# A fused attention, mixture-of-experts and dense kernel: ScalarE's three readings of q are ordered behind the eviction of the value product three pairs ahead

## The chip, the cores and the metric

The kernel is one program on one core of a Trainium2 chip, compiled once. The metric is the device time of one execution in microseconds. The kernel before takes 913.57 us, the median of three runs (913.28 to 913.73). The engines are TensorE (PE, its weight loads PEld), VectorE (DVE), ScalarE (ACT), GpSimd (POOL) and SyncE (SP), which issues most of the transfers.

## What is computed

Three layers follow each other: attention with a compressive memory, a mixture of experts with one expert per token, and a dense layer with a squared relu. The change touches the attention alone, for B=4, H=8, S=576, D=64:

```python
scores = scale * np.matmul(q, k.transpose(0, 1, 3, 2))       # scale = 1/8, causal mask
a = softmax(scores)
local = np.matmul(a, v)                                       # the value product
q_p = np.where(q > 0, q, np.exp(q) - 1.0) + 1.0               # phi(q)
mem_out = (q_p @ M_prev) / (q_p @ z_prev + 1e-6)
attn_out = g * mem_out + (1 - g) * local
```

## The kernel before

**Pairs.** The attention works on 16 pairs of heads (`pair`, 4 batches of 4). Each pair is a Python generator in four parts: "prep" (loads of k and q, their splitting in high and low parts), "front" (scores and their softmax), "back" (turning the weights `a`, the value product, mixing with the memory), "end" (turning the result, routing logits, store). At step t of the main loop, pair t+2 is in prep, t+1 in front, t in back and t-1 in end, interleaved by the table `PLAN`. The program is then put in order by a scheduler that works with estimated durations; `tc.issue_after(x)` around an instruction forbids it to place that instruction ahead of x on its engine.

**Preparation.** For each pair ScalarE copies k into `kh` (L188) and makes `qh` = q/8 (L198), `ex` = exp(q) (L199) and `rq` = relu(q) (L200) from `qraw`, which has two buffers; `qh`, `ql`, `ex` and `rq` have one each. VectorE makes the rest `ql` (L201) and `qpad` = min(ex, 1) + rq (L226), which is phi(q). GpSimd makes `kl` = k - kh (L191) and copies the last 64 queries (`qlasth`, `qlastl`, L214). SyncE copies `qh`, `ql`, `kh` and `kl` into the stacked operands `q2`, `k2`, `qlz`.

**Scores.** `scores((3,))`, `scores((1, 0))` and `scores((2,))` each fill two PSUM banks (tiles `sc3x`, `sc1x`, `sc2x`, one for each head; all are `sc` in the trace). VectorE takes the row maximum (`negm`, L275), ScalarE the exponential (`a`, L278). The last 64 queries of both heads go through `psl` (L287, `al` L288). There are six rotating banks for all tiles made by `bank()`, so each one waits for the eviction of the sixth before it.

**Back.** TensorE turns the weights (`ptl`, `pt`, L76), evicted by `evac` (L171) into `aTs`, ScalarE or VectorE by the table `EV`. The value product is `pva` (L363, 20 matmuls, the columns from 128 on) and `pvb` (L368). ScalarE evicts `pva` into `pvs`, VectorE `pvb`; `c.value` is the eviction of `pva` of the pair that was in back last. The result is turned (`ppt`), scaled by `cl` (L340, L342) into `tl` (L381) and GpSimd adds the memory's part to it (`xb`, L383).

In batch 0 alone, `qh` of a pair is ordered behind `c.value`, which is then the eviction of the pair three places ahead of it; `ex` and `rq` are free everywhere, and `qh` is in the other batches.

Of the kernel before, what the change touches and what calls it, by code (L numbers as in the profile page):

```python
# [14 lines left out]
AF = mybir.ActivationFunctionType  # L15
# [121 lines left out]
def attention(tc, c, q, k, v, x_dram, pools):  # L137
    nc = tc.nc
# [34 lines left out]
    def pair(b, hp, lgT):  # L173
# [6 lines left out]
        def load(nm, src, pool, nb):  # L180
            t = pool.tile([P, S], F32, tag=nm + "raw", name=nm + "raw", bufs=nb)
            nc.sync.dma_start(out=t, in_=src[b, hp])
            return t

        ks = load("k", k, fr, 3)
        qs = load("q", q, fr, 2)
# [7 lines left out]
        ql = fr.tile([P, S], F32R, tag="ql", name="ql", bufs=1)  # L194
        ex = fr.tile([P, S], F32, tag="ex", name="ex", bufs=1)
        rq = fr.tile([P, S], F32, tag="rq", name="rq", bufs=1)
        with tc.issue_after(c.value.ins) if c.value and b == 0 else nullcontext():
            nc.scalar.mul(qh, qs, 0.125)  # L198
        nc.scalar.activation(ex, qs, AF.Exp)  # L199
        nc.scalar.activation(rq, qs, AF.Relu)  # L200
        nc.vector.scalar_tensor_tensor(out=ql, in0=qs, scalar=0.125, in1=qh.bitcast(F32), op0=ALU.mult, op1=ALU.subtract)  # L201
        stacked = b or hp >= NPLAIN

# [237 lines left out]

    order = list(pairs())
    gens = [pair(*o) for o in order]
    n = len(gens)

# [949 lines left out]
```

## Time and profile before

| | |
|---|---|
| median of three runs | 913.57 us (913.28 to 913.73) |
| the profiled execution's own time | 913.89 us |
| its span | 912.2 us, 14430 instructions |
| granted TensorE clock over the span | 0.996 |
| PE / PEld busy | 891.9 us (98%) / 727.3 us (80%) |
| DVE / ACT / POOL busy | 558.4 (61%) / 469.7 (51%) / 191.1 us (21%) |
| the attention's value products | first begins at 26.2 us, the 16th at 220.6 us |

Engine times are shares of a span that holds three stages with different limits; the attention is roughly its first quarter, the rest is experts and dense layer. A busy PE includes the modelled ends of pipelined matmuls, so short waits inside a chain of transposes do not show as idle time. An instruction's time on DVE or POOL includes the time for which it stands at the engine and is kept from its memory port. A releaser is inferred: where an instruction waited for several things, the one that came last is named.

### The profile page before, as it was taken

How to read it: one execution, taken by the hardware profiler on the slowest of the kernel's cores; microseconds unless marked ns; L12 is line 12 of the kernel's file. 1: busy time of each engine (PE TensorE's matmuls, PEld its weight loads, DVE VectorE, ACT ScalarE, POOL GpSimd, SP SyncE). 2: the span in 40 equal slices, each digit the busy share in tenths (PEclk: the TensorE clock that was granted, in tenths of full speed). 3: DMA queues.
4: the chain of work that ended last, by engine and by line, in shares of the span. 5: the costliest groups of instructions: out<-in, count | busy, mean ns of one | idle time of the engine just before them, and what ended most of it. 6: DMA issues, size and time to landing. Idle time of an engine off the chain costs nothing. (4 is left out here: it accounts for less than half of the span.)

```text
span 912.2 us, 14430 instructions
## 1 busy us (share of the span) xinstructions
PE 891.9 (98%) x5208; PEld 727.3 (80%) x5208; DVE 558.4 (61%) x1083; ACT 469.7 (51%) x934; POOL 191.1 (21%) x265
## 2 busy tenths in 40 slices
PE   8899999999989999999999999999999999999998
PEld 5677777777557889889898788888888888888897
DVE  7787988887586887786778699332223222222232
ACT  6788787864445765566566578432222222222232
POOL 6234233423002133054413004130002000100000
PEclk8999999999999999999999999999999999999999
DMA  7987778655647978856761674120002000100010
GB/s 202 219 196 191 192 191 208 157 134 176 202 152 260 353 284 294 295 195 195 247 239 70 238 238 172 35 93 12 12 12 70 1 1 1 46 1 1 3 44 24
DMA packets 81932, 128.97 MB, mean 141 GB/s; under 512 B 9473, under 2 KB 34049, under 8 KB 81857
## 3 DMA queue, kind: packets, MB, share of 16 engines
q1 hardware_dynamic: 76144, 108.86, 39.1%
q0 software_dynamic: 5712, 19.14, 6.4%
q8 instruction: 43, 0.70, 0.3%
q14 instruction: 33, 0.26, 0.1%
HBM read 109.10 MB, written 15.99 MB: 137 GB/s over the span
## 5 line engine op out<-in xcount | busy, mean ns | idle before, releaser
L1232 DVE SCALAR_TENSOR_TENSOR r<-phf,r 128x512 f32<-128x512 f32 (+1 forms) x64 | 40.0, 625 | 176.9 <-ACT r L1230 176.9
L1230 ACT ACTIVATE r<-phf 128x512 f32<-128x512 f32 (+1 forms) x79 | 43.8, 554 | 185.9 <-PE phf L82 181.6
L886 DVE TENSOR_TENSOR wc<-raw,wc 128x1024 fp32r<-128x1024 f32 x91 | 118.3, 1343 | 14.4 <-ACT wc L884 12.9
L80 PE MATMUL phf<-yT,w 128*128 128x512 f32 (+1 forms) x320 | 119.9, 375 | 0.0
L82 PE MATMUL phf<-yT,w 128*128 128x512 f32 (+1 forms) x320 | 118.2, 369 | 1.0 <-DVE w L1140 1.0
L81 PE MATMUL phf<-yT,w 128*128 128x512 f32 (+1 forms) x320 | 117.9, 369 | 0.0
L884 ACT CAST wc<-raw 128x1024 fp32r<-128x1024 f32 x108 | 106.3, 1056 | 18.9 <-DMA raw<-in_w_dram 5.3
L80 PE MATMUL po<-w,gT 128*128 128x512 f32 x256 | 99.8, 391 | 0.3 <-PEq L1102 0.3
L81 PE MATMUL po<-w,gT 128*128 128x512 f32 x256 | 99.8, 390 | 0.0
L82 PE MATMUL po<-w,gT 128*128 128x512 f32 x256 | 92.8, 391 | 0.0
L278 ACT ACTIVATE a<-sc,negm 128x512 f32<-128x512 f32 (+3 forms) x128 | 66.6, 529 | 12.8 <-DVE negm L275 12.8
L80 PE MATMUL py<-wc,hT 128*128 128x512 f32 x176 | 69.9, 397 | 0.2 <-ACT hT L923 0.2
L81 PE MATMUL py<-wc,hT 128*128 128x512 f32 x176 | 68.9, 392 | 0.8 <-DVE wc L886 0.8
L82 PEld LDWEIGHTS phf<-yT,w 128*128 128x128 f32 x320 | 60.2, 188 | 11.7 <-DVE w L1140 1.4
L80 PEld LDWEIGHTS phf<-yT,w 128*128 128x128 f32 x320 | 60.2, 188 | 11.5
L82 PE MATMUL py<-wc,hT 128*128 128x512 f32 x176 | 68.9, 391 | 0.4 <-DVE hT L924 0.4
L81 PEld LDWEIGHTS phf<-yT,w 128*128 128x128 f32 x320 | 60.3, 188 | 10.1
L1237 DVE TENSOR_TENSOR gT<-r,gT 128x512 fp32r<-128x512 f32 x63 | 43.5, 691 | 40.2 <-ACT gT L1236 39.8
L275 DVE TENSOR_REDUCE negm<-sc 128x1 f32<-128x512 f32 (+3 forms) x128 | 55.2, 484 | 19.2 <-PE sc L272 19.1
L886 POOL TENSOR_TENSOR wc<-raw,wc 128x1024 fp32r<-128x1024 f32 x17 | 44.2, 2600 | 90.2 <-ACT wc L884 82.5
L80 PEld LDWEIGHTS po<-w,gT 128*128 128x128 f32 x256 | 48.1, 188 | 10.8 <-issue 0.7
L82 PEld LDWEIGHTS po<-w,gT 128*128 128x128 f32 x256 | 48.0, 188 | 10.3
(358 smaller groups left out, 1953.4 us busy)
## 6 DMA issues: line engine op xcount, KB each, us to landing
raw<-in_w_dram SPq DMA_DIRECT2D x64, 1024.0 KB, 5.4
q<-qh SPq DMA_DIRECT2D x60, 128.0 KB, 2.6
kraw<-in_k_dram SPq DMA_DIRECT2D x16, 288.0 KB, 5.3
qraw<-in_q_dram SPq DMA_DIRECT2D x16, 288.0 KB
vts<-in_v_dram SPq DMA_DIRECT2D x16, 256.0 KB, 3.5
x_dram<-xb SPq DMA_DIRECT2D x16, 256.0 KB, 4.6
k<-kh SPq DMA_DIRECT2D x30, 128.0 KB, 3.2
k<-kl SPq DMA_DIRECT2D x30, 128.0 KB, 2.5
```

Source lines behind the costliest of these rows:

```text
L80: nc.tensor.matmul(out, lhsT=lh, rhs=rh, start=start, stop=False)
L81: nc.tensor.matmul(out, lhsT=lh, rhs=rl, start=False, stop=False)
L82: return nc.tensor.matmul(out, lhsT=ll, rhs=rh, start=False, stop=stop)
L275: nc.vector.tensor_reduce(out=negm[:, h, j:j + 1], in_=psv, axis=AX.X, op=ALU.max, negate=True)
L278: nc.scalar.activation(a[:, h, aoff[j]:aoff[j] + nk], psv, AF.Exp, bias=negm[:, h, j:j + 1], accum_out=ssum[:, h, j:j + 1])
L884: nc.scalar.copy(wc[:, 0, ks], raw[:, ks])
L886: eng.tensor_sub(wc[:, 1, ks], raw[:, ks], wc[:, 0, ks].bitcast(F32))
L1230: nc.scalar.activation(r[:, 0:nt], ph[:, 0:nt], AF.Relu)
L1232: nc.vector.scalar_tensor_tensor(out=r[:, 0:nt], in0=ph[:, 0:nt], scalar=0.0, in1=r[:, 0:nt], op0=ALU.max, op1=ALU.mult)
L1237: nc.vector.tensor_sub(gT[:, 1, 0:nt], r[:, 0:nt], gT[:, 0, 0:nt].bitcast(F32))
```

## The change

The order that held for `qh` in batch 0 now holds for `qh`, `ex` and `rq` in every batch:

```diff
@@ -194,10 +194,10 @@
         ex = fr.tile([P, S], F32, tag="ex", name="ex", bufs=1)
         rq = fr.tile([P, S], F32, tag="rq", name="rq", bufs=1)
-        with tc.issue_after(c.value.ins) if c.value and b == 0 else nullcontext():
+        with tc.issue_after(c.value.ins) if c.value else nullcontext():
             nc.scalar.mul(qh, qs, 0.125)
-        nc.scalar.activation(ex, qs, AF.Exp)
-        nc.scalar.activation(rq, qs, AF.Relu)
+            nc.scalar.activation(ex, qs, AF.Exp)
+            nc.scalar.activation(rq, qs, AF.Relu)
```

No instruction is added or removed; the scheduler places them anew. 13 of the 16 pairs have such a `c.value` to wait for. Below is ScalarE around the value product of the fourth pair (`pva_1097`); `qh_1178`, `kh_1156` and `ex_1180` are of the seventh pair, `ex_1382` and `rq_1383` of the eighth. Before:

```order
L198 ACTIVATE qh_1178<-qraw_1154 128x576
L199 ACTIVATE ex_1382<-qraw_1356 128x576
L200 ACTIVATE rq_1383<-qraw_1356 128x576
L171 COPY pvs1_119<-pva_1097 128x448
L188 CAST kh_1156<-kraw_1152 128x576
L278 ACTIVATE a_962,ssum_961<-sc20_1119,negm_960 128x384
L278 ACTIVATE a_962,ssum_961<-sc21_1120,negm_960 128x384
L171 COPY aTs0_128<-pt00_1203 128x512
```

And with the change:

```order
L171 COPY pvs1_119<-pva_1097 128x448
L198 ACTIVATE qh_1178<-qraw_1154 128x576
L199 ACTIVATE ex_1180<-qraw_1154 128x576
L200 ACTIVATE rq_1181<-qraw_1154 128x576
L188 CAST kh_1156<-kraw_1152 128x576
L278 ACTIVATE a_962,ssum_961<-sc20_1119,negm_960 128x384
L278 ACTIVATE a_962,ssum_961<-sc21_1120,negm_960 128x384
L171 COPY aTs0_128<-pt00_1203 128x512
```

The eviction moved ahead of three activations that now stand between it and `kh`; `ex` and `rq` are of the same pair as `qh`, no longer one pair ahead.

VectorE follows. Around the same value product, before:

```order
L226 SCALAR_TENSOR_TENSOR qpad0_115<-ex_1180,rq_1181 128x576
L355 TENSOR_TENSOR xm_1083<-pm0_1084,cm_1079 128x384
L354 RECIPROCAL cm_1079<-cm_1079 128x4
L355 TENSOR_TENSOR xm_1083<-pm3_1091,cm_1079 128x256
L201 SCALAR_TENSOR_TENSOR ql_1179<-qraw_1154,qh_1178 128x576
L171 COPY pvs1_119<-pvb_1098 128x128
L407 TENSOR_TENSOR lgT_205<-lgT_205,plg_1113 128x160
L275 TENSOR_REDUCE negm_960<-sc20_1119 128x1
L275 TENSOR_REDUCE negm_960<-sc21_1120 128x1
L381 TENSOR_TENSOR tl_1137<-ppt0_1132,cl_1080 128x512
L381 TENSOR_TENSOR tl_1142<-ppt4_1140,cl_1080 128x128
L171 COPY aTs0_128<-ptl_1145 128x2x2x64
```

And with the change:

```order
L407 TENSOR_TENSOR lgT_205<-lgT_205,plg_1113 128x160
L201 SCALAR_TENSOR_TENSOR ql_1179<-qraw_1154,qh_1178 128x576
L275 TENSOR_REDUCE negm_960<-sc20_1119 128x1
L275 TENSOR_REDUCE negm_960<-sc21_1120 128x1
L381 TENSOR_TENSOR tl_1137<-ppt0_1132,cl_1080 128x512
L381 TENSOR_TENSOR tl_1142<-ppt4_1140,cl_1080 128x128
L226 SCALAR_TENSOR_TENSOR qpad0_115<-ex_1180,rq_1181 128x576
L171 COPY aTs0_128<-ptl_1145 128x2x2x64
L340 SCALAR_TENSOR_TENSOR cl_1282<-ssum_961,gneg_235 128x10
L342 RECIPROCAL cl_1282<-cl_1282 128x10
L275 TENSOR_REDUCE negm_1162<-sc30_1214 128x1
```

`ql` moved behind the copy of the logits, and `qpad` from ahead of `xm` to between `tl` and the eviction of `ptl`; behind it stand `cl` and the maximum of the next scores. TensorE's order in these pairs is the same as before, and so is GpSimd's (`qlasth`, `qlastl`, `kl`, `xb`).

## Rows read from the trace of the kernel before

**Rows 1.** Waits, 0 to 240 us: engine, line, releaser: us in total, times, longest.
```profile
ACT ex L199 <- DMA qraw<-in_q_dram: 9.6, 7, 2.9
PE ppt L76 <- ACT pvs L171: 5.2, 4, 2.2
```
**Rows 2.** Timeline of PE, 67 to 83 us: start us, us, what, count.
```profile
67.38 2.70 PE L363 MATMUL pva<-aTs,vts 128*64 128x448 f32 x20
...
71.27 0.34 PE L267 MATMUL sc<-kh,qlz 128*128 128x384 f32 x1
...
72.75 0.38 PE L80 MATMUL psl<-kh,qlasth 128*128 128x288 f32 x1
73.03 0.77 PE L76 MATMUL pt<-ident,a 128*128 128x128 f32 x5
...
77.05 0.39 PE L254 MATMUL sc<-k,q 128*128 128x256 f32 x2
...
79.85 2.70 PE L363 MATMUL pva<-aTs,vts 128*64 128x448 f32 x20
```
**Rows 3.** Timeline of ACT, 68 to 77 us; in brackets the idle time before.
```profile
68.71 0.69 ACT L198 ACTIVATE qh<-qraw 128x576 fp32r<-128x576 f32 x1
69.95 0.68 ACT L199 ACTIVATE ex<-qraw 128x576 f32<-128x576 f32 x1 [0.55 <-DMA qraw<-in_q_dram]
70.54 0.67 ACT L200 ACTIVATE rq<-qraw 128x576 f32<-128x576 f32 x1
71.11 0.51 ACT L171 COPY pvs<-pva 128x448 f32<-128x448 f32 x1
71.64 0.67 ACT L188 CAST kh<-kraw 128x576 fp32r<-128x576 f32 x1
72.31 0.58 ACT L278 ACTIVATE a<-sc,negm 128x384 f32<-128x384 f32 x1
...
75.55 0.69 ACT L278 ACTIVATE a<-sc,negm 128x512 f32<-128x512 f32 x1 [0.80 <-DVE negm L275]
```
**Rows 4.** Timeline of DVE, 69 to 81 us.
```profile
69.49 0.82 DVE L201 SCALAR_TENSOR_TENSOR ql<-qraw,qh 128x576 fp32r<-128x576 f32 x1 [0.17 <-DMA qraw<-in_q_dram]
...
71.72 1.02 DVE L275 TENSOR_REDUCE negm<-sc 128x1 f32<-128x384 f32 x2 [0.62 <-PE sc L272]
72.66 0.88 DVE L381 TENSOR_TENSOR tl<-ppt,cl 128x512 f32<-128x512 f32 x2
73.45 0.41 DVE L171 COPY aTs<-ptl 128x256 f32<-128x256 f32 x1
73.78 0.16 DVE L340 SCALAR_TENSOR_TENSOR cl<-ssum,gneg 128x10 f32<-128x10 f32 x1
73.98 0.22 DVE L342 RECIPROCAL cl<-cl 128x10 f32<-128x10 f32 x1
74.83 1.29 DVE L275 TENSOR_REDUCE negm<-sc 128x1 f32<-128x512 f32 x2 [0.63 <-PE sc L272]
...
80.02 0.75 DVE L226 SCALAR_TENSOR_TENSOR qpad<-ex,rq 128x576 f32<-128x576 f32 x1
```
**Rows 5.** Timeline of POOL, 72 to 76 us.
```profile
72.45 1.41 POOL L191 TENSOR_TENSOR kl<-kraw,kh 128x576 fp32r<-128x576 f32 x1 [1.47 <-issue]
73.82 1.71 POOL L383 TENSOR_TENSOR xb<-tl,xm 128x512 f32<-128x512 f32 x2
```
**Rows 6.** Timelines of POOL and DVE at 14 us and at 216 us.
```profile
14.03 1.40 POOL L191 TENSOR_TENSOR kl<-kraw,kh 128x576 fp32r<-128x576 f32 x1 [1.85 <-ACT kh L188]
...
14.50 1.54 DVE L201 SCALAR_TENSOR_TENSOR ql<-qraw,qh 128x576 fp32r<-128x576 f32 x1
...
215.90 1.69 POOL L383 TENSOR_TENSOR xb<-tl,xm 128x512 f32<-128x512 f32 x2 [9.53 <-DVE tl L381]
...
216.08 1.13 DVE L340 SCALAR_TENSOR_TENSOR cl<-ssum,gneg 128x10 f32<-128x10 f32 x1
```
**Rows 7.** Timeline of PE in a pair with no `psl` product, 132 to 142 us.
```profile
132.79 2.70 PE L363 MATMUL pva<-aTs,vts 128*64 128x448 f32 x20
...
141.87 0.44 PE L254 MATMUL sc<-k,q 128*128 128x256 f32 x2
```

## The prediction

> **What bounds the kernel now.** I read the waits first. In the attention ScalarE waits 9.6 us in front of `ex` for loads of q, and TensorE waits 5.2 us in front of `ppt` for the eviction of the value product [rows 1]. The two belong together: before the change `ex` and `rq` of the next pair stand between the value product and its eviction, and a late load of q holds all three. That is what the change undoes.
>
> Then I read one undisturbed pair in the timeline, engine by engine, because the page's busy share of TensorE hides short waits. The fourth value product ends at 67.38 + 2.70 = 70.08 us [rows 2]. From there a chain runs that is not TensorE's own. `kh` begins at 71.64 [rows 3], when the last score product that reads its buffer has ended, 71.27 + 0.34 = 71.61 [rows 2]. The exponential behind it runs from 72.31 to 72.89 [rows 3], and the transposes that read it begin at 73.03, 0.14 later [rows 2]. One value product to the next takes 79.85 - 67.38 = 12.47 us. So the reader should see that ScalarE's stretch from the value product to the first exponential already decides when TensorE goes on, even where no wait is shown: a microsecond there is a microsecond of the pair.
>
> **The change, part by part.** All 13 pairs with a value product to wait for get the new order. I follow the same pair, on the same clock.
>
> *ScalarE.* Before, `qh` ran at 68.71, while the value product was still going, and cost nothing. Now `pvs` begins at 70.11 (0.03 after its releaser, as `kh` did after 71.61), and `qh`, `ex`, `rq`, `kh` follow. Neighbours overlap by some 0.09 (`ex` lasts 0.68, `rq` begins 0.59 after it [rows 3]). So `qh` begins at 70.53, `ex` at 71.13, `rq` at 71.72, `kh` at 72.30, the exponential at 72.88. It ends at 73.46, and the transposes begin at 73.60 instead of 73.03: **0.57 us later**. `kh` is now bound by ScalarE, no longer by its buffer.
>
> *VectorE and GpSimd.* `kl` follows `kh` by 0.14 (72.45 after 72.31) and takes 1.41 [rows 5]: now from 73.11 to 74.51. `ql` waits for `qh` and runs from 71.25 to 72.07; the two maxima (1.02) and `tl` (0.88) [rows 4] bring VectorE to 73.8. There stands `qpad`, which before ran ahead of the value product, where nobody waited for it. It now meets `kl`, and the trace shows what that means: `ql`, of the same form, began at 14.50 while `kl` ran, and ended at 16.04, 0.61 after `kl` had ended at 15.43; it took 1.54 instead of 0.82 [rows 4, 6]. In the same way `cl`, 0.16 long otherwise, took 1.13 beside `xb` and ended at 217.21; the first of the two `xb` instructions, begun at 215.90, thus takes about 1.28 [rows 4, 6]. The evictions and maxima, which read PSUM, ran beside `kl` and `xb` at their usual length [rows 4, 5].
>
> So `qpad` stands until 74.51 and ends at 75.12. `xb` has been ready since `tl` and takes its turn, 75.12 to 76.40. The eviction of `ptl` runs to 75.45, but `cl` then stands until 76.43; its reciprocal (0.22) ends at 76.69, and the maximum of the next scores begins at 76.61 instead of 74.83. The 0.63 us of idle time that VectorE had there [rows 4], and TensorE's own shift of 0.57, cover only part of that.
>
> *Who waits for that.* The exponential of those scores began 0.72 after the maximum (75.55 after 74.83 [rows 3, 4]): now at 77.33, to 78.02. The score product that TensorE began at 77.05 [rows 2] fills the bank that this exponential empties. It had 0.67 us of room (75.55 + 0.69 + 0.14 = 76.38); now it starts at 78.02 + 0.14 = 78.16, **1.11 us later than before**, and all the rest of the pair with it. The 0.57 is contained in this. Three of the 13 pairs have no `psl` product in this place, so TensorE arrives sooner: 141.87 - 135.49 = 6.38 us after the value product's end [rows 7], where the chain now ends at 78.16 - 70.08 = 8.08. They lose 1.70 each.
>
> For the meeting of `qpad` with `kl`, the page "SBUF — State Buffer" of the Trainium skill has a rule (section Who interferes with whom): a vector instruction with two inputs in SBUF and a GpSimd instruction that reads SBUF share a port, and the loser blocks for the whole instruction. The trace agrees, by the 1.54 and 1.13 us above. By the rule the sum is the one below; without it only the 0.57 would be left.
>
> *SyncE.* The two first copies of `qh` now stand ahead of those of `ql` and `kh`. The number is the same, and their reader is the score product of the next pair's turn, more than 12 us later: nothing. The loads of q stay where they were in the queue and have a pair more to land: the 9.6 us before `ex` vanish.
>
> **The sum.** Ten pairs by 1.11 and three by 1.70 make 16.2 us. From it goes what TensorE waits for the eviction, 5.2 us [rows 1], since `pvs` now runs as soon as the value product ends. That leaves **11.0 us more**. The pairs after a batch's end, with routing work on VectorE, I count like the others; the stages behind the attention are bound by TensorE and simply start later. The profiled execution took 913.89 us, so 924.9 there; it lies 0.32 above the median, against which I forecast **924.6 us**.
>
> *Bounds.* The unknown cost is that of the meeting of VectorE and GpSimd at `kl`'s end. Lower end: it costs nothing, and 13 times 0.57 less 5.2 leaves 2.2 us more, 915.8. Upper end: `xb` goes first, 74.51 to 75.79, then `qpad` to 76.40, and `cl` stands through the second `xb` as well (1.71 - 1.28 = 0.43 long), so it ends 0.43 later than above; pairs lose 1.54 and 2.13, and the sum is 16.6 us, 930.2. I take the middle, since in both meetings that the trace shows the vector instruction that already stood went first: it ended 0.61 and 0.03 after the GpSimd instruction it met [rows 6].
>
> **The rivals.**
> - *Faster: only the gaps count.* The transposes at 73.03 may not wait for the exponential at all: the `psl` matmul in front of them began at 72.75 [rows 2], and 0.28 may just be its length. Then ScalarE has slack behind the value product, `qpad` fits in VectorE's idle 0.63, and what is left is the removed wait: 5.2 us less, 908.4. It decides whether the first exponential may end 0.57 later without TensorE standing. Against it: the 0.14 between exponential and transposes leaves no room. The Trainium skill's page "Perfetto Trace Analysis" (section Optimization Strategy) would lead here: find the gaps on the busiest engine, see what blocks it, and make that start sooner. The gaps shown are just those that the change closes, but the chain that it lengthens shows no gap.
> - *No change to speak of: the ScalarE chain alone.* `qpad` and `cl` slip through between `kl` and `xb`, 915.8. For it: `cl` did slip through before, at 73.78, as `kl` ended. Against it: `qpad` is ready 0.7 us before `kl` ends, and needs 0.75 [rows 4].
> - *Slower still: GpSimd first*, 930.2, as worked out above.
> - That the change does nothing is excluded: the order of the built program shows the new places in all 13 pairs.
>
> **How the numbers follow.** The forecast has 0.72; ScalarE's chain alone 0.11; faster 0.08; GpSimd first 0.09. About 0.2% (1.8 us) can be told from no change, so the chain alone, 2.2 us, lies at the edge: half of it counts as the same, half as slower. That gives faster 0.08, same 0.05, slower 0.87. The range runs from 916, just above the lower bound, to 931, just above the upper one; it leaves out the faster case and about half of the chain alone.
>
> **What would show it.** In the changed profile: no wait of `ppt` for `pvs` and none of `ex` for a load; ScalarE idle before `pvs`, then `pvs`, `qh`, `ex`, `rq`, `kh` without a break; the first exponential about 2.8 us after the value product's end instead of 2.2; `qpad` near 1.4 us long instead of 0.75, `cl` near 1.1; pairs of about 13.6 us instead of 12.47. If `qpad` stays at 0.75 and pairs are about 13.0, the meeting on the port did not happen; if pairs stay at 12.5, ScalarE had slack and the forecast is wrong altogether.

## The result and the profile after

The changed kernel takes **923.05 us** (median of 4 runs, 922.93 to 924.18), the kernel before 913.65 beside it (4 runs): ratio 1.0106, 95% interval 1.0088 to 1.0123, that is 9.4 us slower. The forecast was 11.0 us slower, 924.6. The profiled execution of after took 924.18 us (span 922.5, granted clock 0.994). Its busy times:

```profile
PE 897.8 (97%) x5208; PEld 728.9 (79%) x5208; DVE 569.7 (62%) x1083; ACT 469.0 (51%) x934; POOL 197.9 (21%) x265
```

ScalarE does the same work as before. VectorE and GpSimd are busy 11.3 and 6.8 us longer, though no instruction was added: the rows below show where `qpad`, `cl` and `xb` got longer.

The waits of after, 0 to 245 us (engine, line, releaser: us in total, times, longest):

```profile
ACT pvs L171 <- PE pva L363: 21.9, 15, 2.2
...
PE sc L254 <- ACT a L278: 4.7, 11, 0.9
```

The two waits of [rows 1] are not among them any more: ScalarE now waits for the value product before it evicts it, 15 times, no `ex` waits for a load and no `ppt` for the eviction. A new wait stands on TensorE: a score product waits for the exponential that empties its bank, 11 times.

Now the pair that was followed before. Its value product ends at 68.80 + 2.70 = 71.50 us. ScalarE (start us, us, what, count, and in brackets the idle time before):

```profile
71.55 0.53 ACT L171 COPY pvs<-pva 128x448 f32<-128x448 f32 x1 [1.22 <-PE pva L363]
71.98 0.69 ACT L198 ACTIVATE qh<-qraw 128x576 fp32r<-128x576 f32 x1
72.56 0.68 ACT L199 ACTIVATE ex<-qraw 128x576 f32<-128x576 f32 x1
73.14 0.67 ACT L200 ACTIVATE rq<-qraw 128x576 f32<-128x576 f32 x1
73.71 0.66 ACT L188 CAST kh<-kraw 128x576 fp32r<-128x576 f32 x1
74.28 0.58 ACT L278 ACTIVATE a<-sc,negm 128x384 f32<-128x384 f32 x1
...
78.53 0.69 ACT L278 ACTIVATE a<-sc,negm 128x512 f32<-128x512 f32 x1 [1.26 <-DVE negm L275]
```

The chain runs without a break, as forecast: the first exponential begins 74.28 - 71.50 = 2.78 us after the value product, before 2.23 [rows 2, 3]. VectorE:

```profile
72.76 0.82 DVE L201 SCALAR_TENSOR_TENSOR ql<-qraw,qh 128x576 fp32r<-128x576 f32 x1 [0.23 <-ACT qh L198]
73.50 1.01 DVE L275 TENSOR_REDUCE negm<-sc 128x1 f32<-128x384 f32 x2
74.43 0.87 DVE L381 TENSOR_TENSOR tl<-ppt,cl 128x512 f32<-128x512 f32 x2
75.23 1.31 DVE L226 SCALAR_TENSOR_TENSOR qpad<-ex,rq 128x576 f32<-128x576 f32 x1
76.46 0.41 DVE L171 COPY aTs<-ptl 128x256 f32<-128x256 f32 x1
76.79 0.92 DVE L340 SCALAR_TENSOR_TENSOR cl<-ssum,gneg 128x10 f32<-128x10 f32 x1
...
77.87 1.23 DVE L275 TENSOR_REDUCE negm<-sc 128x1 f32<-128x512 f32 x2
```

GpSimd beside it:

```profile
74.51 1.41 POOL L191 TENSOR_TENSOR kl<-kraw,kh 128x576 fp32r<-128x576 f32 x1 [0.26 <-POOL qlastl L214]
75.88 2.22 POOL L383 TENSOR_TENSOR xb<-tl,xm 128x512 f32<-128x512 f32 x2
```

`qpad` takes 1.31 us instead of 0.75 and ends at 76.54, 0.62 after `kl` (75.92). `xb` is ready, but lets `qpad` pass and takes 2.22 instead of 1.71. `cl` then stands beside `xb` for 0.92 instead of 0.16. Between them lies the eviction of `ptl` at its usual 0.41: it reads PSUM. So the maximum of the next scores begins 77.87 - 71.50 = 6.37 us after the value product, before 74.83 - 70.08 = 4.75. VectorE's 0.63 of idle time there is gone. `qpad` stands in all 13 pairs, `cl` in 11: in the two routing pairs (below) `qpad` stands beside `xb` (1.66 and 1.65) and `cl`, behind it, takes 0.16.

TensorE in this pair, and then in a pair with no `psl` product (its value product starts at 137.65; 132.79 and 145.11 before):

```profile
68.80 2.70 PE L363 MATMUL pva<-aTs,vts 128*64 128x448 f32 x20
...
79.37 0.45 PE L254 MATMUL sc<-k,q 128*128 128x256 f32 x2 [0.17 <-ACT a L278]
...
82.22 0.97 PE L363 MATMUL pva<-aTs,vts 128*64 128x448 f32 x4
```

```profile
137.65 2.70 PE L363 MATMUL pva<-aTs,vts 128*64 128x448 f32 x20
...
143.85 0.76 PE L76 MATMUL pt<-ident,a 128*128 128x128 f32 x5 [0.64 <-ACT a L278]
...
148.21 0.45 PE L254 MATMUL sc<-k,q 128*128 128x256 f32 x2 [0.92 <-ACT a L278]
...
151.45 0.97 PE L363 MATMUL pva<-aTs,vts 128*64 128x448 f32 x4
```

The first pair takes 82.22 - 68.80 = 13.42 us, before 12.47 [rows 2]; the second kind 13.80, before 145.11 - 132.79 = 12.32. In the first the wait shown is 0.17 us of the 0.95 lost: most of that loss stands in no list of TensorE's waits. In the second the waits of 0.64 and 0.92 cover the whole loss of 1.48.

The table gives the time from one value product's start to the next, from the timelines of TensorE, for the runs below too. A pair is numbered by the value product that it starts with. "Ordinary" is pairs 3, 4, 7, 8, 11 and 12, "no `psl`" pairs 5, 9 and 13, "routing" (the routing work of a batch that has ended runs on VectorE) pairs 6 and 10; the last column is from the second value product's start to the sixteenth's.

| kernel, profile | pair 2 | ordinary, each | no `psl` | routing | 2nd to 16th |
|---|---|---|---|---|---|
| before, first profile | 13.71 | 12.46 to 12.52 | 13.06, 12.32, 12.30 | 14.90, 14.67 | 179.4 |
| before again (run 9) | 13.65 | 12.47 to 12.50 | 12.74, 12.27, 12.27 | 13.73, 14.05 | 177.2 |
| after | 13.41 | 13.40 to 13.43 | 13.81, 13.80, 13.81 | 14.79, 14.78 | 188.4 |
| after again (run 10) | 13.41 | 13.40 to 13.43 | 13.80, 13.80, 13.81 | 14.77, 14.77 | 188.4 |
| 1: `qpad` mid | 12.59 | 12.57 to 12.61 | 12.98, 12.98, 12.99 | 15.97, 15.98 | 182.6 |
| 2: after, `qpad` late | 13.01 | 13.01 to 13.05 | 12.80, 12.81, 12.80 | 14.31, 14.29 | 182.4 |
| 3: `ex`, `rq` only | 13.73 | 13.73 to 13.75 | 14.06, 14.05, 14.05 | 15.00, 15.02 | 191.9 |
| 4: `ex`, `rq` behind `xTg` | 12.48 | 12.46 to 12.52 | 12.30, 12.29, 12.27 | 15.28, 16.92 | 180.0 |
| 5: after, `cl` late | 13.03 | 13.00 to 13.03 | 12.80, 12.81, 12.80 | 14.77, 14.77 | 182.4 |
| 8: run 3 with `qpad` late | 12.45 | 12.45 to 12.52 | 12.30, 12.30, 12.29 | 14.63, 14.63 | 177.8 |

The second value product starts at 41.2 and 41.6 us in the two profiles of before, at 42.0 and 41.9 in those of after; over all profiles it lies between 40.0 and 42.9. From there to the sixteenth, after needs 9.0 and 11.2 us more than before's two profiles, 10.1 in the mean. I call that the stretch of the pairs.

### The profile page after: what moved, and what is told of

It is laid out like the page before. It is cut to its first block, busy times and chain, and to the rows that moved or that the text cites. A ratio compares the mean times of both kernels' runs of the same rounds, so it can differ in the third digit from the quotient of the medians.

```text
span 922.5 us, 14432 instructions
## 1 busy us (share of the span) xinstructions
PE 897.8 (97%) x5208; PEld 728.9 (79%) x5208; DVE 569.7 (62%) x1083; ACT 469.0 (51%) x934; POOL 197.9 (21%) x265
## 5 line engine op out<-in xcount | busy, mean ns | idle before, releaser
L886 DVE TENSOR_TENSOR wc<-raw,wc 128x1024 fp32r<-128x1024 f32 x91 | 118.2, 1342 | 14.8 <-ACT wc L884 13.2
L82 PEld LDWEIGHTS phf<-yT,w 128*128 128x128 f32 x320 | 60.2, 188 | 12.1 <-DVE w L1140 1.8
```

Source lines behind the costliest of these rows:

```text
L82: return nc.tensor.matmul(out, lhsT=ll, rhs=rh, start=False, stop=stop)
L886: eng.tensor_sub(wc[:, 1, ks], raw[:, ks], wc[:, 0, ks].bitcast(F32))
```

## The experiments

"Before" took 912.94 us beside runs 1 to 4 (15 runs) and 913.02 beside runs 5 to 8 (23 runs).

**Run 1, VectorE's part of the change alone.** The kernel before, with

```diff
-        nc.vector.scalar_tensor_tensor(out=qpad[i3][:, 0:S], in0=ex, scalar=1.0, in1=rq, op0=ALU.min, op1=ALU.add)
+        with tc.issue_after(c.tl.ins) if c.tl else nullcontext():
+            nc.vector.scalar_tensor_tensor(out=qpad[i3][:, 0:S], in0=ex, scalar=1.0, in1=rq, op0=ALU.min, op1=ALU.add)
```

where `c.tl` is the last product `tl`.

> The kernel before, its ScalarE order kept; alone VectorE's qpad is ordered behind the two tl products, where the change put it. My theory (ScalarE chain plus the meeting of VectorE and GpSimd): qpad stands beside kl, cl beside xb, the maxima of the 512 scores come about 1.0 us later, and as only about 0.6 us of slack lies there, some 0.35 us is lost in each of 8 ordinary pairs and 0.95 in each of 3 pairs without a last-block score product: 913.6 + 5.7 = 919 us (917 to 921). Rival ScalarE chain alone: 913.6. Rival meeting alone: the whole loss is there, 913.6 + 9.4 + 5.2 = 928.

Measured: 917.56 us, ratio 1.0055 (1.0041 to 1.0069). The fourth value product ends at 67.23 + 2.70 = 69.93; VectorE then:

```profile
73.30 1.03 DVE L227 SCALAR_TENSOR_TENSOR qpad<-ex,rq 128x576 f32<-128x576 f32 x1
74.25 0.41 DVE L171 COPY aTs<-ptl 128x256 f32<-128x256 f32 x1
74.59 0.92 DVE L341 SCALAR_TENSOR_TENSOR cl<-ssum,gneg 128x10 f32<-128x10 f32 x1
75.43 1.28 DVE L276 TENSOR_REDUCE negm<-sc 128x1 f32<-128x512 f32 x2
```

Both meetings happen with the short ScalarE chain as well. The maxima begin 5.50 us after the value product, 0.75 later than before, not 1.0; of that, 0.10 us reaches an ordinary pair and 0.67 one with no `psl` product. The order of ScalarE did not stay as I had meant: `ex` has one buffer, must wait for `qpad`, and so moved to 4.5 us after the value product, which took the late load out of the eviction's way too. The two routing pairs lost 1.1 to 2.2 each. So the median fits (919 expected), its parts do only roughly.

**Run 2, the meeting taken out of the change.** The changed kernel, with an extra `yield` ahead of `qpad` and

```diff
+        with tc.issue_after(c.xt.ins) if c.xt else nullcontext():
+            nc.vector.scalar_tensor_tensor(out=qpad[i3][:, 0:S], in0=ex, scalar=1.0, in1=rq, op0=ALU.min, op1=ALU.add)
```

where `c.xt` is VectorE's copy `xTg`.

> The changed kernel, with qpad alone ordered behind VectorE's xTg copy, so that it stands neither beside kl nor ahead of cl and the maxima. My theory: only the ScalarE chain of 0.55 us stays in the pairs, 13.0 us instead of 13.41 in the ordinary ones and 12.9 instead of 13.8 in those without the last-block product: 8 x 0.4 + 3 x 0.95 = 6 us less than the changed kernel, 917 us (915.5 to 918.5). Rival ScalarE chain alone: qpad costs nothing, 923. Rival meeting alone: all of the loss goes and the gain stays, 908.4.

Measured: 918.44 us, 1.0062 (1.0048 to 1.0076). The pairs are about those expected (13.0 and 12.8, expected 13.0 and 12.9), and the stretch is 6.0 us shorter than after's. VectorE, with the value product's end at 68.04 + 2.70 = 70.74:

```profile
74.80 0.40 DVE L343 SCALAR_TENSOR_TENSOR cl<-ssum,gneg 128x10 f32<-128x10 f32 x1
...
76.06 1.29 DVE L278 TENSOR_REDUCE negm<-sc 128x1 f32<-128x512 f32 x2 [0.61 <-PE sc L275]
...
80.74 0.75 DVE L229 SCALAR_TENSOR_TENSOR qpad<-ex,rq 128x576 f32<-128x576 f32 x1
```

`qpad` is back at 0.75, `cl` slips in as `kl` ends, and VectorE waits for TensorE again. What is left, 13.0 against 12.5, is ScalarE's chain: **0.55 us a pair**. In the median 4 of the 6 us arrive; in the profiled run what follows the end of the sixteenth value product took 691.4 us against after's 689.2; why is not shown.

**Run 3, the exponential and the relu alone.** The diff of the change without its first line: `qh` stays under `b == 0`, `ex` and `rq` go behind `c.value`.

> Of the change only the exponential and the relu are ordered behind the value product's eviction; the scaled q is ordered as before. ScalarE's kh then comes about 1.63 us after the value product instead of 2.21, and the first exponential 2.25 after it, as the scores allow anyway; but VectorE's qpad falls between the first maxima and tl, beside kl. My theory: qpad waits for kl until 4.4 us after the product, tl and cl follow, the maxima of the 512 scores begin about 6.5 after it (6.37 in the changed kernel): as slow as the changed kernel, 922 us (920 to 925). Rival ScalarE chain alone: the chain is only 0.07 us longer than before and the wait for the load is gone, 909.5. Rival meeting alone: 922.

Measured: 925.71 us, 1.0142 (1.0126 to 1.0157), slower than the whole change and just above the range expected (920 to 925). The value product ends at 73.10; VectorE and, in the last row, GpSimd:

```profile
75.68 1.87 DVE L227 SCALAR_TENSOR_TENSOR qpad<-ex,rq 128x576 f32<-128x576 f32 x1
77.47 0.87 DVE L382 TENSOR_TENSOR tl<-ppt,cl 128x512 f32<-128x512 f32 x2
...
78.60 0.93 DVE L341 SCALAR_TENSOR_TENSOR cl<-ssum,gneg 128x10 f32<-128x10 f32 x1
...
79.70 1.23 DVE L276 TENSOR_REDUCE negm<-sc 128x1 f32<-128x512 f32 x2
```

```profile
75.53 1.40 POOL L191 TENSOR_TENSOR kl<-kraw,kh 128x576 fp32r<-128x576 f32 x1 [2.33 <-issue]
```

ScalarE's chain is as short as before here (first exponential 2.23 us after the value product), and the pair is the slowest of all: the rival of ScalarE's chain alone, 909.5, is out. `qpad` comes 0.15 us after `kl`'s start instead of 0.72 and takes 1.87; as it stands ahead of `tl`, it delays `tl`, `xb` and `cl`, and the maxima begin 6.60 us after the value product.

**Run 4, `ex` and `rq` where ScalarE has time.** The kernel before; the two activations and `qpad` go behind an extra `yield` and behind ScalarE's last copy `xTg`, some 2 us ahead of the next value product's end:

```diff
-        nc.scalar.activation(ex, qs, AF.Exp)
-        nc.scalar.activation(rq, qs, AF.Relu)
...
+        with tc.issue_after(c.xt.ins) if c.xt else nullcontext():
+            nc.scalar.activation(ex, qs, AF.Exp)
+            nc.scalar.activation(rq, qs, AF.Relu)
```

> The kernel before, with the exponential, the relu and qpad of a pair ordered behind ScalarE's xTg copy, that is some 2 us ahead of the next value product and not between it and the first exponential; the scaled q as before. By then the load has long landed. My theory: the 5.2 us of waits of the eviction go, no pair loses the 0.55 us chain, and qpad lies behind the maxima: 908.4 us (907.5 to 910.5). Rival that the gaps are taken up by something else later: 913.6, no change. Rival meeting alone: 908.4 as well.

Measured: 912.93 us, 0.9997 (0.9988 to 1.0006): no change, the first miss. The pairs without routing are as wished; the two with it are not. There the moved instructions shifted VectorE's small routing operations, and in both pairs `rblk` now meets `kl` (value product's end 145.40; VectorE and GpSimd):

```profile
148.30 1.03 DVE L590 TENSOR_SCALAR rblk<-rs 128x5 int32<-128x5 int32 x1
```

```profile
147.89 1.42 POOL L191 TENSOR_TENSOR kl<-kraw,kh 128x576 fp32r<-128x576 f32 x1 [1.18 <-issue]
```

Five numbers per partition take 1.03 us. Such meetings occur in before as well, with other operations (runs 9 to 11 below). Which of the shifted operations costs these pairs the most was not separated.

**Run 5, `cl` alone taken out of the meeting.** The changed kernel; `cl` and its reciprocal go behind the maxima of the 512 scores (`c.neg` is the last of them):

```diff
+        with tc.issue_after(c.neg.ins) if c.neg else nullcontext():
+            nc.vector.scalar_tensor_tensor(out=cl, in0=ssum, scalar=1e-9, in1=c.gi[:, h0:h0 + 2].unsqueeze(2).to_broadcast((P, 2, NB)),
+                                           op0=ALU.add, op1=ALU.mult)
+            nc.vector.reciprocal(cl, cl)
```

> The changed kernel, with cl and its reciprocal alone ordered behind the two maxima of the 512 scores; qpad stays where the change put it, beside kl. My theory: the maxima no longer stand behind a cl that waits for GpSimd's xb, they begin about 5.3 us after the value product instead of 6.37, and only the ScalarE chain is left: 13.05 us in the ordinary pairs (13.41 in the changed kernel), 12.9 in those without the last-block product (13.8), together 5 us less than the changed kernel: 1.005 of before, 918 us beside 913. Rival, that qpad's own 1.3 us among VectorE's work delays the maxima and not cl's wait: 923.

Measured: 918.08 us, 1.0063 (1.0041 to 1.0085), as expected. The value product ends at 68.72:

```profile
72.45 1.31 DVE L226 SCALAR_TENSOR_TENSOR qpad<-ex,rq 128x576 f32<-128x576 f32 x1
...
74.02 1.29 DVE L275 TENSOR_REDUCE negm<-sc 128x1 f32<-128x512 f32 x2
75.22 0.16 DVE L358 SCALAR_TENSOR_TENSOR cl<-ssum,gneg 128x10 f32<-128x10 f32 x1
```

`qpad` still stands 1.31 us beside `kl`, and it costs nothing: the maxima begin at 5.30, and the ordinary pairs and those with no `psl` are those of run 2 within 0.03 us. So of the two meetings only the second one, `cl` beside `xb`, was late for anybody; the first mattered because it pushed `cl` and `xb` into each other.

**Run 6, the scaled q alone.** The other part of the change: `qh` behind `c.value` in all batches, `ex` and `rq` free.

> Of the change only the scaled q is ordered behind the value product's eviction, in all pairs; the exponential and the relu stay ahead of the eviction, a pair early, as before. My theory: the waits for the load stay; kh comes 1.1 to 1.7 us after the product, early enough, but VectorE's ql moves to where it holds up the first maxima by some 0.3 us in each ordinary pair, and the three pairs with a late load pay 0.57 us for the scaled q: about 913 + 0.3 x 10 + 0.57 x 3 = 917.7 us. Rival ScalarE chain alone: only the three late pairs pay, 914.7.

Measured: 924.38 us, 1.0126 (1.0102 to 1.0150): a miss by 6.7 us. Here the late load and the new chain add up. The second value product ends at 43.22; ScalarE:

```profile
44.69 0.68 ACT L199 ACTIVATE ex<-qraw 128x576 f32<-128x576 f32 x1 [2.71 <-DMA qraw<-in_q_dram]
45.28 0.67 ACT L200 ACTIVATE rq<-qraw 128x576 f32<-128x576 f32 x1
45.85 0.51 ACT L171 COPY pvs<-pva 128x448 f32<-128x448 f32 x1
46.26 0.68 ACT L198 ACTIVATE qh<-qraw 128x576 fp32r<-128x576 f32 x1
46.85 0.66 ACT L188 CAST kh<-kraw 128x576 fp32r<-128x576 f32 x1
48.36 0.58 ACT L278 ACTIVATE a<-sc,negm 128x384 f32<-128x384 f32 x1 [0.85 <-DVE negm L275]
```

A load that is late holds `ex`, `rq`, `pvs`, `qh`, then VectorE's `ql` and the maxima, and the first exponential comes 5.14 us after the value product. Seven of the pairs, the first and the routing pairs among them, take 13.7 to 15.4 us. I had charged the late pairs 0.57 each, as if `ql` behind `qh` did not count there. The waits for q come to 12.1 us (9.6 in before's first profile [rows 1], 11.4 in its second).

**Run 7, run 4 for the first seven pairs alone.** The condition of run 4 with `and b * (H // 2) + hp < 7`.

> The exponential, the relu and qpad ordered behind ScalarE's xTg copy as in the fourth run, but for the first seven pairs alone, before the first pair with routing work; everything behind it is ordered as in the kernel before. In the fourth run the first two late-load pairs took 1.19 and 1.23 us less and the two routing pairs 0.38 and 2.25 more. My theory: the first two gains stay and the routing pairs are as before: 913 - 2.4 = 910.6 us, 0.9974 of before (0.996 to 0.999). Rival, that what is gained early is lost again later: 913.

Measured: 912.58 us, 0.9995 (0.9979 to 1.0012): the gain of 2.4 us is not seen, though the interval leaves room for up to 1.9. In the profile pair 2 takes 12.50 us instead of 13.71, but behind the seventh pair, where the order is that of before, pairs 9 and 10 take 12.74 and 14.79.

**Run 8, both costs out.** Run 3 with run 2's order of `qpad`.

> The third run (the exponential and the relu behind the eviction, the scaled q as before) with qpad ordered behind VectorE's xTg copy as in the second. Both suspected costs are out: the first exponential comes 2.25 us after the product, as early as the scores allow, and qpad stands beside no GpSimd work ahead of the maxima. My theory: ordinary pairs 12.5 us (13.74 in the third run), pairs without the last-block product 12.35 (14.05), and the waits for the load are gone: 913 - 3.2 + 0.5 = 910.5 us (909 to 913). Rival, that the exponential and relu behind the eviction cost by themselves 0.5 us a pair: 917.

Measured: 913.47 us, 0.9998 (0.9986 to 1.0011), outside the 909 to 913 expected: a miss. The pairs are those expected (12.5 and 12.3), no `ex` waits for a load, and the two suspected costs are gone: some 12 us less than run 3 for the order of `qpad` alone. But before is not beaten: its late loads cost it little, and run 8's routing pairs (14.63) and fourteenth pair (13.44 us, 12.70 in before) give that back. None of the kernels run here is shown to beat before.

**Runs 9 to 11, three kernels once more.** Before, after and run 8's kernel, each profiled again, to see what of the profiles repeats.

> The kernel before, unchanged, profiled once more, since the stretch of the 15 pairs took 194.4 us in its one profile and runs that took the late-load waits away gained 2.5 to 3.1 us there and none in the median. Theory A, that the waits for late loads wander from run to run with the transfers: other pairs wait than in the first profile, and the stretch comes out at 191 to 194 us. Theory B, that the waits belong to the order and the gain is lost behind the pairs: the same 194.4 with the same pairs late (14.96, 13.71, 13.06 us for the first, second and fifth), and what follows the last value product takes about 1 us less than in the eighth run (689.5).

> The changed kernel, unchanged, profiled once more. My theory: its pairs wait for no load, so that the 15 pairs take 202.5 us again with the same lengths (13.41, 13.80, 14.78), whatever the loads do; the first value product, which started 1.7 us later than before's ahead of any moved instruction, starts anywhere between 25.7 and 28.9 us, as in the runs so far. Rival, that the later start belongs to the change: 27.9 again.

> The eighth run's kernel, profiled once more. Theory A and B both: the 15 pairs take 191.9 us again, as they wait for no load. Where they differ is the start of the first value product (26.47 in the first profile) and what follows the last (689.5): A expects both to move by about 1 us either way, B expects the same again.

Measured (one execution each: 914.23, 923.85 and 913.64 us): after repeats itself to 0.02 us in every pair from the second on, and run 8's kernel takes 177.6 us from the second value product to the sixteenth (177.8). Before does not repeat: 177.2 against 179.4, mainly in the routing pairs (13.73 and 14.05 against 14.90 and 14.67). Its waits, 0 to 240 us:

```profile
ACT ex L199 <- DMA qraw<-in_q_dram: 11.4, 8, 2.9
...
PE ppt L76 <- ACT pvs L171: 4.3, 4, 2.2
```

Theory B falls, since the stretch is not the same. Theory A holds in part. The same four pairs wait in front of `ppt`, the first two for the same time (2.18 and 1.14 us, 2.19 and 1.18 in the first profile); the other two wait 0.51 and 0.45 instead of 0.82 and 1.05, which is what pairs 5 and 10 got shorter by (0.32 and 0.62). But the largest difference, 1.17 us in pair 6, is no load's: `ex` waits for q there in both profiles, 1.57 us in the first and 1.66 in the second. It is a meeting at `kl`. Before's first profile (VectorE, GpSimd):

```profile
98.29 1.38 DVE L572 TENSOR_TENSOR zs<-zs,so 128x5 f32<-128x5 f32 x1
```

```profile
98.23 1.42 POOL L191 TENSOR_TENSOR kl<-kraw,kh 128x576 fp32r<-128x576 f32 x1 [2.09 <-issue]
```

and its second:

```profile
98.36 0.16 DVE L572 TENSOR_TENSOR zs<-zs,so 128x5 f32<-128x5 f32 x1
```

```profile
98.41 1.42 POOL L191 TENSOR_TENSOR kl<-kraw,kh 128x576 fp32r<-128x576 f32 x1 [2.19 <-issue]
```

Once `zs` begins 0.06 us behind `kl` and stands for 1.38, once it begins 0.05 ahead of it and takes 0.16. A shift of 0.1 us thus decides over a microsecond of the pair.

Two points of what I expected fell. I had counted from the first value product; there after came at 27.8 again, as the rival had it, and its first pair at 14.1, while run 8's first pair took 14.08 once and 16.28 once. So I count from the second value product, which starts between 40.0 and 42.9 us in all thirteen profiles and within 0.1 us in after's two. Whether the 0.3 to 0.8 us by which it is later in after than in before belong to the change stays open. And what follows the end of the sixteenth value product took 690.8 us in before's second profile, 688.6 in its first: it made up for the shorter stretch. Over all profiles it lies between 687.8 and 691.4, so a gain of 2 us in the pairs need not show in one execution's whole; what moves it is open.

## Why the prediction was right, and where its sizes were off

**The sign and the mechanism held.** ScalarE's chain lengthened by 0.55 us (0.57 forecast), runs 2 and 5 show it alone. The pair from which it was read was not quite undisturbed, as `ex` waits 0.55 us for a load in it [rows 3]; but in run 1, where none is waited for there, the first exponential also begins 72.16 - 69.93 = 2.23 us after the value product. `qpad` ended 0.62 after `kl` (0.61), before `xb`, as in the middle case; "GpSimd first" did not happen. The rule of the page "SBUF — State Buffer" of the Trainium skill (section Who interferes with whom), that the loser at the shared port blocks for the whole instruction, agrees with `qpad` at 1.31 and `cl` at 0.92 us, and with 0.75 and 0.16 where nothing of GpSimd's runs beside them. "Only the gaps count" fell: TensorE's 5.2 us went, and the kernel got slower. The Trainium skill's page "Perfetto Trace Analysis" (section Optimization Strategy) advises to find the gaps on the engine that one optimizes, see what blocks it and make that start sooner. Here that alone did not lead to a faster kernel: the gaps of 5.2 us were closed, and pairs whose TensorE had shown no gap lost 0.93 us each.

**The loss of a pair, forecast at 1.11 and 1.70 us, measured 0.93 and 1.50.** The step in which `cl` stands until 76.43, 6.35 us after the value product, was mis-sized: it ended 6.21 after it (77.71). `xb` was taken to need its full 1.28 us after `qpad`; measured from `qpad`'s end (76.54) to `cl`'s, it needed 1.17. So the maxima came 1.62 us later instead of 1.78. The room of 0.67 that the forecast gave the score product is confirmed from two sides: 1.62 - 0.67 = 0.95 in after (0.93 measured), 0.75 - 0.67 = 0.08 in run 1 (0.10).

**The gain, forecast at 5.2 us, was about 2, an estimate from the pairs.** That step took TensorE's waits in front of `ppt` at their face value. In before they are four, and here are the three ahead of 90 us:

```profile
32.48 0.66 PE L76 MATMUL ppt<-ident,pvs 128*128 128x128 f32 x4 [2.19 <-ACT pvs L171]
...
46.84 0.66 PE L76 MATMUL ppt<-ident,pvs 128*128 128x128 f32 x4 [1.18 <-ACT pvs L171]
...
85.14 0.66 PE L76 MATMUL ppt<-ident,pvs 128*128 128x128 f32 x4 [0.82 <-ACT pvs L171]
```

The first shows no gain: in the profiles without it the second value product starts at 40.0 to 42.9 us, in before at 41.2 and 41.6. The second is worth 1.2 (13.71 to 12.45 in run 8), the third 0.8 or, in run 9, 0.4. The fourth lies in a routing pair (pair 10), whose length wandered by 0.6 us between two profiles of the same kernel; no run separates what it is worth, and it is not counted. Run 2 agrees: it has ScalarE's chain without the meeting, for which the prediction's lower end was 2.2 us more, and lies 5.5 above before; 13 times 0.57 less 2 is 5.4.

**The routing pairs were not like the others, and the first pair shows no loss.** Counted at 1.11 each, the routing pairs came out at 14.8 us in after, 0 and 1.8 us more in sum than in before's two profiles. `cl` stands beside nothing there, and run 5, which moves it, leaves them at 14.77. The first pair was counted at 1.11 as well; it ends within the spread of the other kernels.

Sum of what was measured, against before's first profile: six ordinary pairs at 0.93 make 5.6, three with no `psl` 3.7 net of the late load, pair 2 -0.3, the routing pairs 0.0: 9.0 us from the second value product to the sixteenth. Against the second profile it is 5.6 + 4.1 - 0.2 + 1.8 = 11.2, with rounding. The medians, 9.4 apart, lie between. A gain some 3 us too large and a loss 3 to 5 us too large met in a forecast that is 1.6 us too high: that it came so close is in part luck. That the stages behind the attention simply start later held within their spread: 689.2 and 689.0 us in after, 688.6 and 690.8 in before.

## What to carry to other kernels

Before moving work off one engine's wait, look where it lands on each of the others: here three activations went from a place with slack to the head of the chain that decides when the next pair starts, and a product that follows them fell beside GpSimd work. A wait that the busiest engine shows is worth at most its length, and nothing where something else holds the next step; to price one, take it out in a run of its own. A profile is one draw where instructions wait for loads or reach a shared port at nearly the same time: here two of four waits repeated and two did not, and 0.1 us decided a meeting worth more than 1 us. Take a second profile before counting such times as a gain.

## What the runs showed of the hardware that was not expected

- At the port between VectorE and GpSimd the vector instruction that already stood there went ahead of GpSimd's next one each time: `qpad` ahead of `xb` in after and in runs 1 and 5, `cl` between `kl` and `xb` in run 2 (0.40 us), `cl` between the two `xb` instructions in after (0.92).
- How long a vector instruction stands goes by the rest of the GpSimd instruction that it meets, not by its own size: 5 numbers per partition took 1.03 us in run 4 and 1.38 in before, 10 took 0.92 in after. The maxima and evictions, which read PSUM, kept their length beside the same instructions (the eviction of `ptl` 0.41).
- An instruction that is late at the port is free as long as what stands behind it has room: 0.56 us of `qpad` in run 5 cost nothing, while 0.76 us of `cl` in after cost 0.4 us in an ordinary pair (13.41 against 13.02) and 1.0 in one with no `psl` product (13.80 against 12.80).
